# Second product of the experts in PSUM tags c and d, all row numbers read first, three decoded pairs kept in the ring

## The chip, the cores and the metric

The kernel runs on one core of one Trainium2 chip. The metric is device time in microseconds, the median of several executions of the same kernel on the same chip. One more execution is profiled; it has its own time and its own span, and every row below is from it.

## The reference

Attention over a window, then a mixture of experts with one expert for each token, then a dense layer with a squared relu:

```python
B, H, S, D = (4, 8, 576, 64)            # attention, window 128, ALiBi slopes
attn = softmax(mask(scale * q @ k.T + bias)) ; x = (attn @ v).transpose(0, 2, 1, 3).reshape(2304, 512)
expert_idx = np.argmax(x @ w_gate, axis=1)              # 8 experts, softmax weight gate_w
for e in range(8):
    mask = expert_idx == e
    h = np.maximum(x[mask] @ w1[e], 0.0)                # 512 -> 1024
    out[mask] = gate_w[mask, None] * (h @ w2[e])        # 1024 -> 512
r = np.maximum(out @ w_in, 0.0)                         # moe2: 512 -> 2048
y = (r * r) @ w_out                                     # 2048 -> 512
```

All inputs are float32 but `w_in` and `w_out`, which come as 64-bit floats and are decoded on the chip. Products are made of float16 halves, a high and a low part of each operand.

## The kernel before

The program has three stages: attention to about 160 us of the span, the eight experts from about 180 to 402 us, and the dense layer, called moe2 here, to the end. It is written as one stream of instructions for tiles; a scheduler sorts it into one queue for each engine, and each engine works through its queue in order. A tile of a pool waits until the last reader of the buffer's former tile is done.

Pools and buffers that the change touches:

- PSUM has four tags a, b, c, d with two banks each (`psum`, L131).
- `wr` (`ring`, L116) is a ring of 12 buffers for split weights, `rw` (`raw`, L128) has 4 buffers for raw loads, `xg` 6 buffers for gathered rows. `dec` is one buffer in which 64-bit words are decoded.
- `wi_s` holds the decoded `w_in` in 8 tiles, `wi_3345` to `wi_3352` in the rows. Until its own data is made, the last four also serve as staging: for raw expert weights (`stage`, L761) and for decoded pieces of `w_out` on their way to DRAM.

An expert e works as follows. `prep` (L986) reads the row numbers of its tokens from a list in DRAM into `idt`, `gather` (L993) clips them on POOL and fetches the rows by indirect DMA into `xg`. `turn` (L998) transposes each block of rows on TensorE into tag d (`transpose_x`, L791), and ACT copies it to `xt`. `s1` (L798) makes the first product in eight pieces fc with banks from a and b in turn; ACT and DVE take each result to float16 halves (L807, L808). `s2` (L849) adds up the second product over the same eight pieces in four accumulators, of tags c, c, a, b, and ACT copies them to `yT` after the last piece (L863). Weights come by SP's queue (`raw_w`, L756); ACT makes the high half (L778) and DVE the low half (L779) of each of the four pieces of `w1` and of `w2`.

Between these steps, at places named by a table (`STEPS`), the program decodes `w_in` and `w_out`: `wide` (L936) ends the step before and begins the next. A step of `w_out` (`out_step`, L916) loads 512 KB, decodes it on DVE (L880 to L882) and splits it (ACT L927, DVE L928). Eight steps are first: their results, of the list `SENT`, go into staging parts of `wi_3349` to `wi_3352`, are stored in DRAM (`wod`, L931) and are fetched when moe2 begins (`fetch_out`, L966). Then come sixteen steps of `w_in` and eight of `KEPT`, whose results stay in ring buffers.

The rows for the first experts are read late in the routing: `prep(0)` and `prep(1)`, then `gather(0)` and `gather(1)`, then three late scatters that put the gate's weights of the last tokens into the list; `prep(e + 2)` and `gather(e + 2)` are called in `then` during the second product of expert e. In moe2, `wide1` (L1191) makes 2 or 4 ring buffers of squared values for a group of 256 tokens (L1210, L1211).

Of the kernel before, what the change touches and what calls it, by code (L numbers as in the profile page):

```python
# [56 lines left out]
SENT = (4, 5, 12, 13, 6, 7, 14, 15)  # L57
# [36 lines left out]
class K:  # L94
# [754 lines left out]
    def s2(self, ws, hts, at, n, then=None):  # L849

        nc = self.nc
        ys = [self.psum(t, [P, n]) for t in "ccab"]
        for fc in range(8):
            hh, hl = hts[fc][:, 0, :n], hts[fc][:, 1, :n]
            for d, py in enumerate(ys):
                o = fc % 2 * DM + d * P
                wh, wl = (ws[fc // 2][:, a, o:o + P] for a in range(2))
                nc.tensor.matmul(py, wh, hh, start=fc == 0, stop=False)  # L858
                nc.tensor.matmul(py, wl, hh, start=False, stop=False)  # L859
                self.last_mm = nc.tensor.matmul(py, wh, hl, start=False, stop=fc == 7)  # L860
            if fc == 7:
                for d, py in enumerate(ys):
                    nc.scalar.copy(self.yT[:, d, bass.ds(at, n)], py)  # L863
            if then is not None and fc % 2 == 1:
                then(fc // 2)
# [50 lines left out]
    def out_step(self, fc):  # L916

        nc = self.nc
        f = self.wide_load(self.wo, [(slice(fc * P, (fc + 1) * P), lambda r, k: r, DM, lambda st, k: st)])

        def finish():
            if fc in KEPT:
                dst = self.wo_s[fc]
            else:
                dst = self.wi_s[4 + SENT.index(fc) % 4].rearrange("p k a c -> p (k a c)")[:, 2048:3072].rearrange(
                    "p (a d) -> p a d", a=2)
            nc.scalar.activation(dst[:, 0], f, AF.Copy, scale=WOSC)  # L927
            nc.vector.scalar_tensor_tensor(dst[:, 1], f, WOSC, dst[:, 0], op0=ALU.mult, op1=ALU.subtract)  # L928
            if fc not in KEPT:
# [20 lines left out]
    def open_wide(self, stack):  # L950
# [4 lines left out]
        self.steps = [(self.out_step, fc) for fc in SENT] + \  # L955
# [16 lines left out]
    def experts(self, stack):  # L972
# [31 lines left out]
        prep(1)  # L1004
# [11 lines left out]
        for e in range(E):  # L1016
# [10 lines left out]
            for fc in range(8):  # L1027
# [10 lines left out]
                if fc in (3, 5, 7) and more:  # L1038
                    turn(nxt, e + 1, fc // 2 - 1)
# [3 lines left out]
            def then(d):  # L1043
                if more:
                    w[2, e + 1, d] = self.load_w(2, e + 1, d)
                if e + 2 < E:
                    if d == 0:
                        prep(e + 2)
# [9 lines left out]
                if d == 3 and e < 7:  # L1058
                    self.columns(e)
                    if e == 6:  # L1060
                        self.columns(7)

            self.narrow = e == 6
# [127 lines left out]
    def wide1(self, G, m, between=lambda k: None):  # L1191
# [9 lines left out]
        g = self.gts[G, m] = [self.ring(F16, [P, 2, 8 * P]) for _ in range(n)]  # L1201
# [178 lines left out]
    def moe2(self):  # L1380
        NG, tc = NT // GT, self.tc
        self.overflow()
        nrm = {1: self.norm(1, 7168, None)}
        next(nrm[1])
# [106 lines left out]
```

## Time and profile before

| | |
|---|---|
| median of 3 runs | 748.61 us (748.33, 748.61, 751.21) |
| profiled execution | 751.45 us, span 749.6 us |
| PE busy | 712.6 us (95%) |
| weight loads (PEld) | 603.5 us (81%) |
| DVE busy | 576.8 us (77%) |
| ACT busy | 468.8 us (63%) |
| POOL busy | 206.5 us (28%) |
| mean granted clock of TensorE | 0.984 |

A busy time is the sum of an engine's instructions, and matmuls overlap each other, so that PE's 95% is no measure of waits: those stand in the waits and in the brackets of the timeline. A bracket such as `[1.82 <-DVE work L808]` says how long the engine stood idle before the row, and which instruction or transfer ended the wait. In the windows the granted clock is a share of full speed: 1.0 is 2.4 GHz and 0.5 is 1.2 GHz. The 1.8 us between the profiled time and the span lie before and after the span. The profiled execution is 2.84 us above the median of the runs.

### The profile page before, as it was taken

The numbers are of one execution on the slowest core, as the hardware profiler recorded it, in microseconds if no ns is written. First come the engines' busy times: TensorE is split into PE (matmuls) and PEld (weight loads), VectorE is DVE, ScalarE is ACT, GpSimd is POOL, SyncE is SP. The second block draws the span as 40 slices with busy tenths as digits, with TensorE's granted clock in tenths as the row PEclk, the third lists the DMA queues.
The fourth block names the chain that finished last, engine by engine and source line by source line (L and its number), as shares of the span: only waits on it lengthen the run. The fifth ranks groups of instructions, "written<-read, shape, count | busy, mean of one in ns | idle before, by whom it ended". The sixth has DMA issues, their size and how long they took to land. (4 is left out here: it accounts for less than half of the span.)

```text
span 749.6 us, 19619 instructions
## 1 busy us (share of the span) xinstructions
PE 712.6 (95%) x7979; PEld 603.5 (81%) x7979; DVE 576.8 (77%) x1442; ACT 468.8 (63%) x772; POOL 206.5 (28%) x247
## 2 busy tenths in 40 slices
PE   6899999999888999999999999999999999999996
PEld 5799899888655666788898566677899999999995
DVE  5788888864778999969986966758678787878672
ACT  5688888943457655657555664656657575757561
POOL 4573522345252401000000245523411111111011
PEclk9899999989999999999999999999999999999998
DMA  8798203876899887367704000000000000000000
GB/s 299 289 365 234 81 29 68 278 163 172 239 305 299 283 263 240 125 220 241 241 5 141 31 26 6 2 30 1 30 2 30 2 30 2 30 2 30 2 30 29
DMA packets 37416, 91.71 MB, mean 122 GB/s; under 512 B 5305, under 2 KB 16075, under 8 KB 37307
## 3 DMA queue, kind: packets, MB, share of 16 engines
q1 hardware_dynamic: 31563, 75.77, 32.1%
q0 software_dynamic: 5760, 14.65, 6.0%
q8 instruction: 64, 1.05, 0.6%
q14 instruction: 29, 0.24, 0.1%
HBM read 77.54 MB, written 13.04 MB: 121 GB/s over the span
## 5 line engine op out<-in xcount | busy, mean ns | idle before, releaser
L1187 PEld LDWEIGHTS <-wi 128*128 128x128 f16 x3024 | 170.6, 98 | 3.6 <-issue 2.3
L1323 PEld LDWEIGHTS <-wr 128*128 128x128 f16 x1008 | 98.1, 98 | 12.1 <-issue 0.7
L1187 PE MATMUL ps_a<-work,wi 128*128 128x128 f16 x1344 | 84.2, 219 | 0.0
L1187 PE MATMUL ps_b<-work,wi 128*128 128x128 f16 x1272 | 79.7, 219 | 0.4 <-ACTq L1075 0.4
L1211 DVE TENSOR_TENSOR wr<-work,wr 128x1024 f16<-128x1024 f32 (+1 forms) x72 | 70.4, 1001 | 11.0 <-ACT wr L1210 10.8
L1215 ACT ACTIVATE work<-work 128x1024 f32<-128x1024 f32 x36 | 38.1, 1057 | 54.8 <-DVE work L1207 54.8
L315 PE MATMUL ps_a<-yT,wr 128*128 128x192 f32 (+2 forms) x288 | 66.6, 352 | 5.4 <-DMA wr<-in_q_dram 5.2
L1210 ACT CAST wr<-work 128x1024 f16<-128x1024 f32 (+1 forms) x72 | 59.9, 832 | 17.1 <-DVE work L1230 7.6
L327 ACT ACTIVATE pb<-pb,nm 128x192 f32<-128x192 f32 (+2 forms) x144 | 56.5, 433 | 11.6 <-DVE nm L320 10.8
L320 DVE CUSTOM_DVE_ANT_0 pb<-ps_a,bias 128x192 f32<-128x192 f32 (+2 forms) x144 | 44.4, 327 | 16.1 <-PE ps_a L315 10.2
L778 ACT ACTIVATE wr<-rw 128x1024 f16<-128x1024 f32 x40 | 42.2, 1058 | 22.1 <-DMA rw<-in_w_dram 21.5
L1351 POOL DMA_INDIRECT out_dram<-o,oid x18 | 25.8, 1436 | 102.0 <-ACT o L1349 67.4
L779 DVE SCALAR_TENSOR_TENSOR wr<-rw,wr 128x1024 f16<-128x1024 f32 x40 | 48.8, 1221 | 5.0 <-ACT wr L778 5.0
L315 PEld LDWEIGHTS ps_a<-yT,wr 128*128 128x128 f32 x288 | 47.1, 206 | 6.4 <-DMA yT<-in_k_dram 5.5
L1286 POOL TENSOR_TENSOR yT<-wr 128x512 f32<-128x512 f16 x8 | 10.4, 1294 | 148.9 <-ACTq L1075 116.0
L338 PE MATMUL ps_b<-cst,pb 128*128 128x128 f32 x256 | 45.1, 288 | 0.5 <-ACT pts L342 0.4
L804 PE MATMUL ps_a<-work,wr 128*128 128x352 f16 (+4 forms) x112 | 34.1, 304 | 7.0 <-ACT yT L863 5.6
L1216 ACT ACTIVATE work<-work 128x1024 f32<-128x1024 f32 x36 | 38.0, 1057 | 1.1
L787 POOL DMA_INDIRECT xg<-xd,idx x21 | 26.8, 1274 | 35.6 <-PE ps_d L795 26.5
L1235 DVE TENSOR_TENSOR work<-work 128x512 f32<-128x512 f32 x18 | 13.3, 739 | 29.8 <-ACT work L1204 29.8
L859 PEld LDWEIGHTS <-wr 128*128 128x128 f16 x288 | 28.2, 98 | 9.8 <-issue 2.6
L858 PE MATMUL ps_c<-work,wr 128*128 128x352 f16 (+5 forms) x128 | 35.9, 283 | 0.0
(307 smaller groups left out, 2005.8 us busy)
## 6 DMA issues: line engine op xcount, KB each, us to landing
rw<-in_w_dram SPq DMA_DIRECT2D x40, 512.0 KB, 5.4
wi<-in_w_dram SPq DMA_DIRECT2D x20, 512.0 KB, 5.0
rw<-in_wo_dram SPq DMA_DIRECT2D x16, 512.0 KB, 4.7
rw<-in_wi_dram SPq DMA_DIRECT2D x32, 256.0 KB, 5.2
wr<-in_q_dram SPq DMA_DIRECT2D x14, 512.0 KB, 12.8
xd<-xhl POOLq DMA_DIRECT2D x16, 256.0 KB, 7.8
rw<-in_v_dram SPq DMA_DIRECT2D x12, 325.0 KB, 6.4
yT<-in_k_dram SPq DMA_DIRECT2D x4, 576.0 KB, 8.7
```

The lines of the kernel that those rows point to most:

```text
L315: nc.tensor.matmul(ps[:, s, first:hi], q[g, u, hh // 4][:, hh % 4, s if u < 4 else 0, :], self.kt[g, hh // 2][:, hh % 2, key0:key0 + hi - ...
L320: self.last_ttr = nc.vector.tensor_tensor_reduce(out=pb[:, s, first:hi], in0=ps[:, s, first:hi], in1=self.bias[:, hh, first - lo:192], sca ...
L327: self.last_exp = nc.scalar.activation(pb[:, s, first:hi], pb[:, s, first:hi], AF.Exp, bias=nm[:, s:s + 1], scale=-1.0)
L338: nc.tensor.transpose(pt[:, t, :, s, :], pb[:, s, t * P:(t + 1) * P], self.idf)
L778: self.nc.scalar.activation(t[:, 0], st, AF.Copy, scale=sc)
L779: self.nc.vector.scalar_tensor_tensor(t[:, 1], st, sc, t[:, 0], op0=ALU.mult, op1=ALU.subtract)
L1187: self.nc.tensor.matmul(ps[:, j], w[:, kp, a, w0 * P:(w0 + 1) * P], v[:, 2 * x + kp], start=kp + b == 0, stop=kp == 1 and b == 2)
L1210: self.end_act = self.fin_act = nc.scalar.copy(hi, src)
L1211: self.end_dve = self.fin_dve = V.tensor_tensor(lo, src, hi, op=ALU.subtract)
L1215: nc.scalar.activation(ci, ci, AF.Relu)
L1216: nc.scalar.activation(ci, ci, AF.Square, scale=0.5)
L1323: nc.tensor.matmul(ps[n], x[:, v, j], y[j][:, w], start=m + i + j == 0, stop=m == 1 and i == 2 and j == 3)
```

## The change

Seven edits:

1. `s2` uses tags c, c, d, d; `s1` has a and b alone, and the transposes share d with `s2`.
2. From expert 1 on, the transposes for the next expert follow pieces 2, 4 and 6 of `s1` instead of 3, 5 and 7.
3. `prep` is called for all eight experts at the start, ahead of both gathers and of the late scatters.
4. The copies of the row lists (`columns`) are called at the end of experts 5 and 6.
5. Six decoded pieces of `w_out`, the list `HELD`, are written straight to three buffers of the ring, which they keep; only pieces 14 and 15 are stored in DRAM and fetched again. Nine ring buffers are left for the experts' weights.
6. For the later groups of moe2, three of four buffers of squared values come from `rw`.
7. `wide1(0, 0)`, which is made in expert 7, uses banks a and b alone.

```diff
-SENT = (4, 5, 12, 13, 6, 7, 14, 15)
+HELD = (4, 5, 12, 13, 6, 7)
+SENT = (14, 15)
...
-        ys = [self.psum(t, [P, n]) for t in "ccab"]
+        ys = [self.psum(t, [P, n]) for t in "ccdd"]
...
+        if fc in HELD and fc not in self.wo_s:
+            for _ in self.wo_tiles((fc, fc + 1), lambda: self.ring(F16, [P, 2048])):
+                pass
...
-            if fc in KEPT:
+            if fc not in SENT:
...
-            if fc not in KEPT:
+            if fc in SENT:
...
-        self.steps = [(self.out_step, fc) for fc in SENT] + \
+        self.steps = [(self.out_step, fc) for fc in HELD + SENT] + \
...
-        prep(1)
+        for e in range(1, E):
+            prep(e)
...
-                if fc in (3, 5, 7) and more:
-                    turn(nxt, e + 1, fc // 2 - 1)
+                if more and fc in ((3, 5, 7) if e == 0 else (2, 4, 6)):
+                    turn(nxt, e + 1, (fc + 1) // 2 - (2 if e == 0 else 1))
...
-                    if d == 0:
-                        prep(e + 2)
...
-                if d == 3 and e < 7:
-                    self.columns(e)
-                    if e == 6:
-                        self.columns(7)
-
-            self.narrow = e == 6
+                if d == 3:
+                    for f in {5: range(6), 6: (6, 7)}.get(e, ()):
+                        self.columns(f)
+
+            self.narrow = e >= 6
...
-        g = self.gts[G, m] = [self.ring(F16, [P, 2, 8 * P]) for _ in range(n)]
+        spare = 3 if n == 4 and m == 0 else 0
+        g = self.gts[G, m] = [self.ring(F16, [P, 2, 8 * P]) for _ in range(n - spare)] + \
+            [self.rw.tile([P, 2048], F16, tag="rw", name="rw").rearrange("p (a n) -> p a n", a=2) for _ in range(spare)]
...
+        self.narrow = False
```

The order of instructions moves on three queues of which the prediction speaks. Line numbers of the changed kernel are 1 higher than before up to about L916 and 3 to 4 higher behind it.

POOL, from the row numbers to the first gathers (`ids` is the list in DRAM, `idx` the clipped row numbers, `xd` the rows). Before:

```order
L989 DMA ids<-ids 128x2
L989 ISA
L989 DMA ids<-ids 128x3x2
L995 TENSOR_SCALAR idx<-ids 128x1
L787 DMA xg<-xd,idx 128x1024
L995 TENSOR_SCALAR idx<-ids 128x3
L787 DMA xg<-xd,idx 128x1024 x3
```

Now, from the fourth reading on:

```order
L993 DMA ids<-ids 128x3x2
L993 ISA
L993 DMA ids<-ids 128x3x2
L993 ISA
L993 DMA ids<-ids 128x2x2
L993 ISA
L993 DMA ids<-ids 128x2x2
L993 ISA
L993 DMA ids<-ids 128x2x2
L999 TENSOR_SCALAR idx<-ids 128x1
L999 TENSOR_SCALAR idx<-ids 128x3 x3
L788 DMA xg<-xd,idx 128x1024 x4
```

Six more readings, and the clipping for experts 2 and 3, now stand ahead of the first gather; two gathers for expert 2 follow the late scatters at once.

SP, the loads and stores while expert 1's second weights are fetched (`rw` and `wi_3349` receive raw weights, `wod` receives decoded `w_out`). Before, from the store of the fifth decoded piece to that of the seventh:

```order
L931 DMA wod<-wi_3349 128x1024
L756 ISA
L756 DMA rw<-in_w_dram 128x1024
L931 DMA wod<-wi_3350 128x1024
L756 ISA
L756 DMA rw<-in_w_dram 128x1024
L756 ISA
L756 DMA rw<-in_w_dram 128x1024
L756 ISA
L756 DMA rw<-in_w_dram 128x1024
L931 DMA wod<-wi_3351 128x1024
L756 ISA
```

Now:

```order
L757 DMA rw<-in_w_dram 128x1024
L935 DMA wod<-wi_3349 128x1024
L757 ISA
L757 DMA wi_3349<-in_w_dram 128x1024
L876 DMA rw<-in_wi_dram 128x2x256 x2
L757 ISA
L757 DMA rw<-in_w_dram 128x1024
L935 DMA wod<-wi_3350 128x1024
L876 DMA rw<-in_wi_dram 128x2x256 x2
L757 ISA
L757 DMA wi_3350<-in_w_dram 128x1024
```

Before, `wi_3349` and `wi_3350` were stored for the last time several loads ahead of their use as staging; now the store of each stands one or a few rows ahead of the load into it.

ACT, the last rows ahead of the copies to `yT` of expert 1. Before:

```order
L778 ACTIVATE wr<-wi_3352 128x1024
L911 ACTIVATE wi_3345<-dec 128x896
L778 ACTIVATE wr<-rw 128x1024
L778 ACTIVATE wr<-wi_3349 128x1024
L863 ISA
L863 COPY yT<-ps_c 128x384
```

Now:

```order
L779 ACTIVATE wr<-wi_3352 128x1024
L912 ACTIVATE wi_3345<-dec 128x896
L864 ISA
L864 COPY yT<-ps_c 128x384
L864 ISA
L864 COPY yT<-ps_c 128x384
L864 ISA
L864 COPY yT<-ps_d 128x384
```

Two splits of expert 2's second weights, which stood ahead of the copies, now follow them.

## Rows read from the trace of the kernel before

**Rows 1.** waits of TensorE: engine line waited for: us in total, times, longest us

```profile
PE ps_a L804 <- ACT yT L863: 5.6, 4, 2.1
...
PE ps_d L795 <- DMA xg<-xd,idx: 3.8, 2, 3.4
...
PE ps_b L858 <- DVE work L808: 2.2, 2, 1.8
```

**Rows 2.** stages: us, PE PEld DVE ACT POOL busy (x), PEclk, DMA share, GB/s

```profile
195.50:236.80 41.30, 36.11 (x230) 21.68 (x228) 31.50 (x50) 22.25 (x32) 18.82 (x25) 0.96 0.94 304
236.80:269.80 33.00, 30.89 (x212) 20.09 (x211) 31.87 (x64) 21.83 (x32) 10.46 (x8) 0.95 0.83 275
...
348.50:372.20 23.70, 22.73 (x221) 20.10 (x220) 22.77 (x44) 14.77 (x25) 0.00 (x0) 1.00 0.79 249
372.20:402.50 30.30, 28.10 (x360) 27.68 (x360) 24.17 (x43) 17.37 (x33) 0.00 (x0) 1.00 0.07 21
402.50:470.00 67.50, 64.24 (x730) 46.30 (x731) 49.09 (x84) 37.70 (x50) 26.18 (x26) 1.00 0.16 56
```

**Rows 3.** TensorE timeline, expert stage: start us, us, line, tiles [idle before <-releaser]

```profile
206.21 0.72 PE L795 MATMUL ps_d<-id,xg 128*128 128x128 f16 x8 [3.37 <-DMA xg<-xd,idx]
...
220.38 0.32 PE L858 MATMUL ps_b<-work,wr 128*128 128x384 f16 x1 [1.82 <-DVE work L808]
...
240.37 0.31 PE L804 MATMUL ps_a<-work,wr 128*128 128x352 f16 x1 [2.11 <-ACT yT L863]
...
273.50 0.31 PE L804 MATMUL ps_a<-work,wr 128*128 128x352 f16 x1 [1.41 <-ACT yT L863]
...
373.78 0.26 PE L804 MATMUL ps_a<-work,wr 128*128 128x224 f16 x1 [1.66 <-ACT yT L863]
```

**Rows 4.** windows around three waits: us, PE busy, granted clock (1 is full speed)

```profile
206.20:210.00 3.80, 3.79 (x19) 0.55 0.87 251
...
240.40:244.10 3.70, 3.70 (x14) 0.54 0.57 150
...
273.50:277.00 3.50, 3.50 (x24) 1.00 0.92 250
```

**Rows 5.** POOL timeline, start of the experts

```profile
169.60 1.42 POOL L989 DMA_DIRECT2D ids<-ids  x2 [4.65 <-DMA ids<-tok,pos]
174.97 0.24 POOL L995 TENSOR_SCALAR idx<-ids 128x1 uint32<-128x1 f32 x1 [3.95 <-DMA ids<-ids]
175.76 1.07 POOL L787 DMA_INDIRECT xg<-xd,idx  x1 [0.56 <-POOL idx L995]
...
195.30 0.82 POOL L989 DMA_DIRECT2D ids<-ids  x1 [8.01 <-DMA ids<-tok,pos]
...
201.35 1.06 POOL L787 DMA_INDIRECT xg<-xd,idx  x1 [0.36 <-POOL idx L995]
```

**Rows 6.** TensorE timeline, start of the experts

```profile
180.92 0.62 PE L795 MATMUL ps_d<-id,xg 128*128 128x128 f16 x8 [0.45 <-DMA xg<-xd,idx]
```

**Rows 7.** ACT timeline, experts 0 and 1

```profile
182.48 0.63 ACT L927 ACTIVATE wi<-dec 128x512 f16<-128x512 f32 x1
...
225.41 1.06 ACT L778 ACTIVATE wr<-wi 128x1024 f16<-128x1024 f32 x1 [3.43 <-DMA wi<-in_w_dram]
...
239.09 0.84 ACT L863 COPY yT<-ps_c 128x384 f32 x2
```

**Rows 8.** SP timeline, the DMA issues of expert 1

```profile
207.96 0.39 SPq L756 DMA_DIRECT2D wi<-in_w_dram  x1
...
219.21 1.29 SPq L756 DMA_DIRECT2D wi<-in_w_dram  x1
```

**Rows 9.** DMA issues: count, KB each, median us from issue to landing

```profile
wod<-wi SPq DMA_DIRECT2D x8, 256.0 KB, 4.7
...
ids<-ids POOLq DMA_DIRECT2D x4, 3.0 KB, 5.4
```

## The prediction, on record before the changed kernel ran

> **What bounds the kernel now.** I read the waits of TensorE first, because its queue is full from end to end and the time is its matmuls plus its waits and slow stretches. In the experts stage three kinds of wait hold nearly all of what this change can reach [rows 1]: the first product waits for the copies to `yT` (5.6 us in four waits), the transposes wait for gathered rows (3.8 us in two), and the second product waits for DVE to free bank b (2.2 us in two). The windows by stage say what surrounds them [rows 2]. In expert 1 the DMA engines are busy 0.94 of the time and DVE 31.5 of 41.3 us; in expert 2 DVE is busy 31.9 of 33.0 us; from 402 us on PE is the bound (64.2 of 67.5 us), and there the change does nearly nothing.
>
> The timeline shows the five large waits singly [rows 3]: 3.37 us for rows of expert 2 at 206.2, 1.82 us at 220.4, 2.11 us at 240.4, 1.41 us at 273.5 and 1.66 us at 373.8, together 10.4 us. Behind two of them the granted clock falls from its upper level of 2.4 GHz to about 1.2 GHz: 0.55 over 3.8 us behind the first and 0.54 over 3.7 us behind the third, but 1.00 behind the wait of 1.41 us [rows 4]. Each dip costs 3.8 x 0.45 = 1.7 us of work. So all that could go is 10.4 + 3.4 = 13.8 us. The question is how much of it is only cover for something that is late anyway.
>
> **Start of the experts: the row numbers.** Two readings took POOL 1.42 us, the first was waited for 3.95 us, and the first gather was issued at 175.76 [rows 5]. Now eight readings stand first. POOL needs 8 x 0.75 = 6 us for them, until 175.6. That alone moves the gather by 0.6 us, for POOL used to sit idle here. But the clipping for experts 2 and 3 also stands ahead of the first gather, so it waits until the fourth reading has landed. That one is issued at about 172 and lands 3.95 [rows 5] to 5.4 us later [rows 9], so about 177.2. With 0.8 us for the last clipping and the gap that follows, the gather goes out at 178.0, 2.2 us later. TensorE was already waiting 0.45 us for gathered rows at 180.9 [rows 6], so little hides this: I take **+1.9 us**, between 0.6 (POOL's time alone) and 4.3 (a landing of 8.01 us, the longest wait for this list in the trace [rows 5]). What it buys: the reading for expert 2 was issued only at 195.3, behind the late scatters, and its first gather at 201.35 [rows 5]; two of the three gathers now go out at about 190, and the 3.37 us with its dip, **-5.1 us**, goes.
>
> **Expert 1: the decoded pieces in the ring.** The ACT half of the first `w_out` step ran at 182.48 [rows 7] into a staging tile that was free. Now it needs a ring buffer, and the first comes free when the first pair of pieces of expert 0's first product is done, about 3.7 us after that product begins (181.4 before). Eight steps go one behind another through the one `dec` buffer, so the steps, and behind them on ACT and DVE the splits of expert 1's second weights, come about 3.6 us later. On ACT the copy of the last transposes for expert 2 stands among these splits, and until it is done they hold the second d bank, which the second product now needs. I put that copy at 219.3. The wait of 1.82 us for bank b, which ended at 220.38 [rows 3], so becomes a wait for bank d that ends about 1.1 us sooner and is longer (TensorE arrives some 5 us earlier), and may bring a dip of 1.7 us with it. Up to here the gain is between -1.1 and +0.6 us.
>
> **Expert 2: the stores.** Six of eight stores of 256 KB go. The two that are left now stand right ahead of raw loads into the same tiles: the loads issued at 207.96 and 219.21 [rows 8] must wait until the store has landed, 4.7 us [rows 9]. With the 3.6 us of the steps ahead I put them at 216 and 223.5. ACT's split at 225.41 waited 3.43 us for the first of these loads [rows 7]; it comes at 228 to 230.5. Behind it on ACT stand five more splits and then the copies to `yT`, which began at 239.09 [rows 7]; two splits of 1.06 us that stood ahead of them now follow. So the first d bank is copied between 238.5 and 242.3, and only then can the transposes behind piece 2 start. Piece 4 of expert 2 begins at 244.3 to 247.8, against 246.07 before. I take the middle: at this point the change is worth **0 us**, between -1.8 and +1.7, and the first three waits with their dips have been eaten by the chain of loads and splits behind them.
>
> Against that stands the traffic: six stores of 256 KB are 1.57 MB, 5.2 us at the 304 GB/s of a stage in which the DMA engines are busy 0.94 of the time [rows 2]. SP's issues wait for free buffers more than for the engines, so I take **-1.0 us** of it, between 0 and -5.2.
>
> The trace's store lands in 4.7 us. The Trainium skill (DMA: Bandwidth & Descriptors, Anatomy of one DMA) puts a transfer at some 2.0 us plus its bytes at 436 GB/s, most of it the write receipt, which makes an estimated 2.6 us for 256 KB; by that the two loads would be 2.1 us sooner and the whole sum -4.5 us. The measured 4.7 us decides here.
>
> **Experts 3 to 7.** The waits for the copies at 273.5 (1.41 us) and in expert 6 (the fourth of [rows 1], 5.6 - 2.11 - 1.41 - 1.66 = 0.4 us) go, since `s1` has a and b for itself; the transposes behind piece 2 ask for d about 1.7 us later than the old wait began, when the copies are done or nearly so: **-1.9 us**, between 0 and -2.2. Expert 7's 1.66 us goes too, but a step of `KEPT` w_out slips from before the copies of expert 6 to behind them, on a DVE that had 24.2 us to do in 30.3 us and now gets up to 5 more [rows 2], and bank a is still held there by the norm's product. I take **+0.5 us** in all, between -1.7 and +1.5.
>
> **At nothing** stand: three fetches fewer at the start of moe2 and three buffers from `rw` for later groups (a PE-bound stage), the copies of the lists (POOL is idle beyond 240 us), and `wide1(0, 0)` in two tags, as DVE paces it. If `rw` came free late, a wait there would be new.
>
> **Sum:** 0 - 1.0 - 1.9 + 0.5 = -2.4 us. Against the profiled execution that is 751.45 - 2.4 = 749.05 us; that execution lies 2.84 us above the median of 748.61, so I predict **746.2 us**. About 0.5%, 3.7 us, is what a measurement of this kernel can tell from no change.
>
> **Rivals.**
> *The engines of the DMA were the bound.* For: 0.94 busy, and the waits of ACT for loads in expert 1 are long. Against: loads are issued when a buffer comes free. Then the 5.2 us come off the chain in full: -2.4 - 4.2 = -6.6 us, 742.0, and down to 739 if the d copies keep up too. 0.27.
> *The waits only change their name.* DVE is nearly full in experts 2 and 6 (31.9 of 33.0 and 22.8 of 23.7 us) [rows 2]; PE would wait for DVE's half of each piece instead of the copies. Then nothing comes of experts 3 to 6 and of the relief: 0 + 0.5, 749.1, no change. 0.15.
> *The row numbers make the start late, and the kernel slower.* In order on POOL, the first gather waits for the fourth reading. If that lands 8.0 us after its issue as in [rows 5], the gather goes at 180.4, TensorE is late by 4.4 instead of 1.9 us and a dip of 1.7 us follows: 4.2 us more. The ring buffers come free with the same matmuls, so the chain moves with it and no later slack takes it back; with the chain at its late end (+1.7) and no relief (+1.0) the sum is +4.5 us, 753.1. It decides from a first gather behind 180 on; at 178 it is covered. 0.13.
> That the change does not do what it says (a, b still shared) is excluded by the order of the queues shown with it.
>
> **Numbers.** The forecast has 0.45, with a range of its own from 743.5 to 749.5. The 8-in-10 range leaves out the lowest part of the first rival and the upper half of the last: 740.5 to 751.0. Faster by over 0.5% (under 744.9): most of the first rival, 0.26, and a quarter of the forecast, 0.11, with 0.02 of the second: 0.39. Slower by over 0.5% (above 752.3): most of the last, 0.09, and 0.02 of the rest: 0.11. Within: 0.50.
>
> **What would show it.** Right: the first gather at about 178; no wait for rows at expert 2's transposes; a wait of the second product for bank d until about 219; the wait of `s1` for `yT` gone from the list, with one of the transposes for `yT` in its place at about 241; piece 4 of expert 2 at 246 ± 2 us. The forecast is wrong if expert 2 begins more than 3 us sooner (the first rival), if waits for DVE take up the gain from expert 3 on (the second), or if the first gather comes behind 180 (the last).

## The result: slower, and the profile after

The changed kernel takes 756.51 us (median of 754.93, 755.77, 757.25 and 759.49), the kernel before 749.91 us in the runs beside it (748.33 to 751.58): a ratio of 1.0103, with a 95% interval from 1.0077 to 1.0128. That is slower by 1%, and outside the predicted range (740.5 to 751.0 us). The profiled execution took 754.93 us, span 753.1, the fastest of the four; against the first profiled execution it is 3.5 us longer.

The waits of TensorE, changed kernel, to be read against [rows 1] (engine, line waited for: us in total, times, longest us):

```profile
PE ps_a L805 <- DVE work L809: 6.4, 2, 3.5
...
PE ps_d L859 <- ACT work L797: 4.0, 2, 3.9
PE ps_a L805 <- DVE yT L1143: 3.4, 1, 3.4
...
PE ps_d L796 <- DMA xg<-xd,idx: 0.9, 1, 0.9
...
PE ps_d L796 <- ACT yT L864: 0.6, 1, 0.6
```

What the change was to remove is gone: the first product waits for no copy to `yT`, the transposes wait for gathered rows for 0.9 us only, at the start of the experts, and the second product not at all for DVE. Others stand in their place: the copy of transposes out of tag d (L797, 4.0 us in two), and on DVE its half of a piece of the first product (L809, 6.4 us in two) and the product of the first norm (L1143, 3.4 us).

The TensorE timeline gives the four large waits, against [rows 3] (start us, us, line, tiles [idle before <-releaser]):

```profile
216.61 0.48 PE L859 MATMUL ps_d<-work,wr 128*128 128x384 f16 x1 [3.85 <-ACT work L797]
...
303.44 0.29 PE L805 MATMUL ps_a<-work,wr 128*128 128x304 f16 x1 [2.88 <-DVE work L809]
...
356.06 0.37 PE L805 MATMUL ps_a<-work,wr 128*128 128x256 f16 x1 [3.50 <-DVE work L809]
...
379.76 0.35 PE L805 MATMUL ps_a<-work,wr 128*128 128x224 f16 x1 [3.43 <-DVE yT L1143]
```

And windows behind each of them, against [rows 4] (us, PE busy, granted clock, DMA share, GB/s):

```profile
216.60:220.40 3.80, 3.79 (x12) 0.50 0.70 194
...
303.40:307.00 3.60, 3.56 (x23) 0.64 0.26 61
...
356.00:359.60 3.60, 3.54 (x25) 0.58 0.52 154
...
379.70:383.30 3.60, 3.54 (x21) 0.55 0.63 249
```

All four are followed by the lower clock level for most of 3.6 to 3.8 us. Taken as the share of full speed that is missing, that is 1.9, 1.3, 1.5 and 1.6 us of work. In the kernel before, two waits were followed by a dip [rows 4].

Where the time went is seen best from the start of each expert's first product on TensorE's timeline:

| us of the span | before | after | difference |
|---|---|---|---|
| expert 1 | 194.88 | 194.29 | -0.6 |
| expert 2 | 234.52 | 233.64 | -0.9 |
| expert 3 | 268.34 | 263.51 | -4.8 |
| expert 4 | 299.86 | 293.75 | -6.1 |
| expert 5 | 325.66 | 324.15 | -1.5 |
| expert 6 | 348.66 | 346.00 | -2.7 |
| expert 7 | 373.78 | 373.87 | +0.1 |
| moe2 | 403.27 | 407.23 | +4.0 |

So the change does gain 6 us, by expert 4. Three waits of 2.88, 3.50 and 3.43 us in experts 4, 6 and 7, with 4.4 us of work lost to the slow clock behind them, give back over 10. By stages, against [rows 2] (us, then PE, PEld, DVE, ACT, POOL busy, clock, DMA share, GB/s):

```profile
194.00:231.00 37.00, 33.15 (x209) 19.73 (x207) 29.18 (x45) 19.74 (x31) 12.74 (x15) 0.91 0.85 282
231.00:263.00 32.00, 32.00 (x231) 21.27 (x229) 30.85 (x67) 21.17 (x31) 3.87 (x3) 1.00 0.83 280
263.00:295.60 32.60, 32.35 (x236) 21.65 (x235) 28.28 (x49) 19.65 (x31) 4.01 (x3) 1.00 0.62 199
...
345.00:375.00 30.00, 25.95 (x241) 22.68 (x240) 25.05 (x47) 18.77 (x32) 0.00 (x0) 0.94 0.71 223
```

In the stage of expert 1 the DMA engines are now 0.85 busy, not 0.94. DVE is not fuller than before; in the stage of the wait at 356 it has 25.0 of 30.0 us to do, against 22.8 of 23.7 [rows 2]. It is late, not overloaded.

**Why DVE is late in expert 4.** ACT's and DVE's timelines of the changed kernel at the wait, first ACT, then DVE:

```profile
294.63 1.08 ACT L779 ACTIVATE wr<-rw 128x1024 f16<-128x1024 f32 x1
300.90 0.95 ACT L912 ACTIVATE wi<-dec 128x896 f16<-128x896 f32 x1 [5.18 <-DVE dec L907]
301.75 0.41 ACT L808 ACTIVATE work<-ps_a 128x304 f16<-128x304 f32 x1
```

```profile
288.28 1.22 DVE L780 SCALAR_TENSOR_TENSOR wr<-wi,wr 128x1024 f16<-128x1024 f32 x1
...
293.65 1.22 DVE L780 SCALAR_TENSOR_TENSOR wr<-wi,wr 128x1024 f16<-128x1024 f32 x1
297.93 0.43 DVE L881 TENSOR_SCALAR dec<-rw 128x512 uint32<-128x512 uint32 x1 [3.06 <-DMA rw<-in_wi_dram]
...
302.92 0.47 DVE L809 SCALAR_TENSOR_TENSOR work<-ps_a,work 128x304 f16<-128x304 f32 x1
```

ACT stood still for 5.18 us. It had reached the ACT half of a `w_in` step (L912), which waited for DVE's decode, and DVE's decode (L881) had waited 3.06 us for its load. Behind L912 in ACT's queue stood the relu of expert 4's first piece (L808), whose result had long been in bank a; DVE's half (L809) followed at 302.92. The same step before, the tenth of `w_in` in both kernels, on ACT:

```profile
301.73 0.95 ACT L911 ACTIVATE wi<-dec 128x896 f16<-128x896 f32 x1 [2.06 <-DVE dec L906]
...
304.22 0.42 ACT L807 ACTIVATE work<-ps_a 128x304 f16<-128x304 f32 x1
```

It ran at 301.73, 0.8 us later than now, and waited 2.06 us. TensorE had come 6 us forward, the step had not. Its load was issued at 290.50, right behind a load of expert weights (SP's timeline of the changed kernel; the rows at 207 belong to a point below):

```profile
207.51 0.34 SPq L935 DMA_DIRECT2D wod<-wi  x1
208.05 0.34 SPq L757 DMA_DIRECT2D wi<-in_w_dram  x1
...
289.52 0.34 SPq L757 DMA_DIRECT2D wi<-in_w_dram  x1
...
290.50 1.21 SPq L876 DMA_DIRECT2D rw<-in_wi_dram  x2
```

That load of weights (289.52) stood 7.3 us on SP. The profile puts the wait down to DVE, and the split of a staged buffer (L780, from 288.28 to 289.50) ended just as the load went out. So there is a loop through three queues that each work in order: a step waits for its load, the load stands on SP behind a load of weights, that one waits for a split, and the split stands on ACT and DVE behind the step before. The loads of `w_in` went out at 270.1, 279.8, 286.5 and 293.5 before, one in 7.8 us on average; now at 271.6, 281.0, 290.5 and 299.8, one in 9.4.

**Why DVE is late in expert 6.** DVE's timeline of the changed kernel:

```profile
354.11 0.43 DVE L881 TENSOR_SCALAR dec<-rw 128x512 uint32<-128x512 uint32 x1 [0.75 <-DMA rw<-in_wi_dram]
354.45 1.22 DVE L780 SCALAR_TENSOR_TENSOR wr<-rw,wr 128x1024 f16<-128x1024 f32 x1
355.59 0.42 DVE L809 SCALAR_TENSOR_TENSOR work<-ps_a,work 128x256 f16<-128x256 f32 x1
```

ACT's relu of the piece had begun at 353.35. DVE's half of it stood behind the first row of a decode, which waited for its load, and behind a split.

**Why DVE is late in expert 7.** DVE's timeline, changed kernel, then before:

```profile
375.68 0.43 DVE L881 TENSOR_SCALAR dec<-rw 128x512 uint32<-128x512 uint32 x1 [0.38 <-DMA rw<-in_wo_dram]
...
376.75 1.22 DVE L780 SCALAR_TENSOR_TENSOR wr<-rw,wr 128x1024 f16<-128x1024 f32 x1
...
378.49 1.21 DVE L1143 TENSOR_TENSOR yT<-yT,ps_a 128x1024 f32<-128x1024 f32 x1
```

```profile
374.14 0.69 DVE L881 SCALAR_TENSOR_TENSOR dec<-rw,dec 128x512 uint32<-128x512 uint32 x1
...
375.47 1.21 DVE L1141 TENSOR_TENSOR yT<-yT,ps_a 128x1024 f32<-128x1024 f32 x1
```

The norm's product frees bank a for piece 2 of expert 7. It stands behind the decode of a `w_out` step and a split and came at 378.49, against 375.47 before.

### The profile page after: what moved, and what is told of

Read it like the earlier page. It is cut to its first block, busy times and chain, and to the rows that moved or that the text cites. A ratio compares the mean times of both kernels' runs of the same rounds, so it can differ in the third digit from the quotient of the medians.

```text
span 753.1 us, 19622 instructions
## 1 busy us (share of the span) xinstructions
PE 712.0 (95%) x7979; PEld 601.8 (80%) x7979; DVE 577.5 (77%) x1442; ACT 467.4 (62%) x772; POOL 200.4 (27%) x247
## 5 line engine op out<-in xcount | busy, mean ns | idle before, releaser
L1189 PE MATMUL ps_b<-work,wi 128*128 128x128 f16 x1320 | 82.7, 219 | 0.3 <-PEq L1077 0.3
L316 PE MATMUL ps_a<-yT,wr 128*128 128x192 f32 (+2 forms) x288 | 65.0, 346 | 5.5 <-DMA wr<-in_q_dram 5.3
L1327 PEld LDWEIGHTS <-wr 128*128 128x128 f16 x648 | 63.4, 98 | 8.2 <-issue 0.7
L1215 DVE TENSOR_TENSOR wr<-work,wr 128x1024 f16<-128x1024 f32 (+1 forms) x48 | 48.8, 1037 | 11.2 <-ACT wr L1214 11.0
L1290 POOL TENSOR_TENSOR yT<-wr 128x512 f32<-128x512 f16 x10 | 12.7, 1267 | 167.2 <-ACTq L1077 128.3
L780 DVE SCALAR_TENSOR_TENSOR wr<-rw,wr 128x1024 f16<-128x1024 f32 x40 | 48.7, 1218 | 5.2 <-ACT wr L779 5.1
L1355 POOL DMA_INDIRECT out_dram<-o,oid x18 | 23.6, 1309 | 103.3 <-ACT o L1353 46.0
L1214 ACT CAST wr<-work 128x1024 f16<-128x1024 f32 (+1 forms) x48 | 42.5, 885 | 8.2 <-DVE work L1234 4.2
L859 PE MATMUL ps_d<-work,wr 128*128 128x352 f16 (+5 forms) x128 | 36.5, 288 | 4.0 <-ACT work L797 4.0
L860 PEld LDWEIGHTS <-wr 128*128 128x128 f16 x288 | 28.5, 99 | 12.3 <-issue 5.4
L1327 PEld LDWEIGHTS <-rw 128*128 128x128 f16 x360 | 34.8, 98 | 3.8
L788 POOL DMA_INDIRECT xg<-xd,idx x21 | 24.4, 1164 | 46.5 <-PE ps_d L796 25.5
```

The lines of the kernel that those rows point to most:

```text
L316: nc.tensor.matmul(ps[:, s, first:hi], q[g, u, hh // 4][:, hh % 4, s if u < 4 else 0, :], self.kt[g, hh // 2][:, hh % 2, key0:key0 + hi - ...
L780: self.nc.vector.scalar_tensor_tensor(t[:, 1], st, sc, t[:, 0], op0=ALU.mult, op1=ALU.subtract)
L1189: self.nc.tensor.matmul(ps[:, j], w[:, kp, a, w0 * P:(w0 + 1) * P], v[:, 2 * x + kp], start=kp + b == 0, stop=kp == 1 and b == 2)
L1214: self.end_act = self.fin_act = nc.scalar.copy(hi, src)
L1215: self.end_dve = self.fin_dve = V.tensor_tensor(lo, src, hi, op=ALU.subtract)
L1327: nc.tensor.matmul(ps[n], x[:, v, j], y[j][:, w], start=m + i + j == 0, stop=m == 1 and i == 2 and j == 3)
```

## The experiments

Ratios are to the kernel before on the same chip, in runs taken beside each other. The kernel before itself had medians from 748.8 to 752.5 us on the chips used, so that times from different chips are not compared. The changed kernel was timed on one chip, in the four executions above, and not again beside its variants. Theories, in short: 1, the ring of nine buffers makes loads and steps late; 2, the new order of copies and steps on ACT, which comes with the banks, makes the waits. The expected microseconds were given for a kernel before of 749 to 750 us.

### The parts alone

**Without the held pieces** (edits 5 and 6 undone, all else kept):

```diff
-HELD = (4, 5, 12, 13, 6, 7)
-SENT = (14, 15)
+SENT = (4, 5, 12, 13, 6, 7, 14, 15)
...
```

> The changed kernel with eight w_out pieces stored and fetched as before and all 12 ring buffers for the experts' weights (buffers of the later groups of moe2 from the ring again); banks, early transposes and early row numbers stay. Theory 1 (the ring of 9 makes splits, loads and so the w_in steps late): 739 to 744 us, 6 to 10 less than before, the three new waits of 2.9 to 3.5 us in experts 4, 6 and 7 gone. Theory 2 (the new order of copies and w_in steps on ACT, which comes with the banks, makes the waits): 753 to 758 us, the waits stay.

Measured: 759.23 us, ratio 1.0108 (1.0054 to 1.0163). Theory 1 fails as the whole answer: with all twelve buffers back the kernel is as slow as with nine. Its waits, and one of them on TensorE's timeline:

```profile
PE ps_d L858 <- ACT work L796: 6.6, 4, 4.0
PE ps_a L804 <- DVE work L808: 5.5, 5, 2.9
...
PE ps_a L804 <- DVE yT L1139: 3.2, 1, 3.2
```

```profile
244.06 0.31 PE L804 MATMUL ps_a<-work,wr 128*128 128x352 f16 x1 [2.92 <-DVE work L808]
```

But the time goes elsewhere. In experts 4 and 6, where the changed kernel waited 2.88 and 3.50 us for DVE, no such wait is over 1 us here, as theory 1 had it. Expert 2 takes 38.5 us from start to start instead (changed kernel 29.9, before 33.8), with waits of 2.9 us for DVE and 2.1 us for a copy of transposes. Of the four large waits, those for the copy of transposes in expert 1 (4.0 us) and for the norm in expert 7 (3.2 us) are in both.

**Held pieces alone** (edits 5 and 6 on the kernel before):

> The kernel before with the six pieces kept in the ring and nothing else but the buffers of moe2 that this needs. Theory 1: 753 to 760 us, w_in steps from the eighth on 4 to 8 us later, in experts 4 to 7 new waits of TensorE for DVE. Theory 2: 747 to 751 us, no such waits.

Measured: 755.56 us, ratio 1.0065 (1.0039 to 1.0091), with waits of 1.8 us for DVE in expert 4 and 4.5 us for a copy to `yT` in expert 6. Loads of `w_in` at 270.8, 280.4, 289.4, 298.6, the cadence of the changed kernel. Theory 1 holds for this part.

**Banks and transposes alone** (edits 1, 2 and 7 on the kernel before):

```diff
-        ys = [self.psum(t, [P, n]) for t in "ccab"]
+        ys = [self.psum(t, [P, n]) for t in "ccdd"]
...
-                if fc in (3, 5, 7) and more:
...
+                if more and fc in ((3, 5, 7) if e == 0 else (2, 4, 6)):
...
-            self.narrow = e == 6
+            self.narrow = e >= 6
...
```

> The kernel before with c, c, d, d, the earlier transposes and the narrow first product of moe2 in expert 7. Theory 1: 744 to 748 us; the waits for the copies to yT go, the wait for gathered rows of expert 2 stays or grows by the piece that the transposes come sooner. Theory 2: 752 to 757 us with new waits in experts 4 to 7.

Measured: 757.10 us, ratio 1.0102 (1.0049 to 1.0156). Here loads of `w_in` are not late (326.7 and 353.5 for the thirteenth and the sixteenth, 326.1 and 353.0 before). Its waits:

```profile
PE ps_d L795 <- DMA xg<-xd,idx: 4.0, 1, 4.0
...
PE ps_d L858 <- ACT work L796: 3.4, 2, 3.1
PE ps_a L804 <- DVE yT L1141: 3.1, 1, 3.1
```

The rows of expert 2 are waited for 0.6 us longer, as the transposes ask sooner; the second product waits 3.1 us for a copy of transposes out of tag d, in expert 2; the norm's wait of 3.1 us in expert 7 is there. Theory 2 had the time about right, and of its new waits in experts 4 to 7 the norm's is the only large one: most of the loss is in expert 2, which takes 37.1 us against 33.8 before.

**Row numbers alone** (edits 3 and 4 on the kernel before):

```diff
-        prep(1)
+        for e in range(1, E):
+            prep(e)
...
-                    if d == 0:
-                        prep(e + 2)
...
```

> The kernel before with all row numbers read at the start and the list copies late. Both theories: the wait of 3.37 us for rows of expert 2 and its slow stretch go. Theory 1: 744 to 748 us, of which some is given back at the copies of expert 1. Theory 2 says the same here or no change, 747 to 750 us.

Measured: 752.86 us, ratio 1.0040 (1.0015 to 1.0065). The 3.37 us for rows go, and the second product of expert 1 waits for DVE instead, 3.5 us at 216.9 and 1.4 us at 219.4. Both theories expected a gain or no change; every part alone costs.

**The ring alone** (the kernel before with three ring buffers held idle from the start of the experts to expert 6):

```diff
+        full = [self.ring(F16, [P, 2048]) for _ in range(3)]
+        for t in full:
+            nc.gpsimd.memset(t[:, :2], 0.0)
...
+            if e == 6:
+                m7 = xgs[7][0].shape[0]
+                for t in full:
+                    nc.gpsimd.tensor_copy(t[:m7, 2:4], xgs[7][0][:, :2])
```

> The kernel before with three ring buffers taken out of use from the start of the experts to expert 6 (each is written once and read once) and nothing else: stores, banks and row numbers as before. If the smaller ring is what makes the w_in loads late in the kernel with held pieces alone: 752 to 758 us, and the loads of w_in from the ninth on are issued 4 to 8 us later, some 9 us apart. If it is the order of steps around the held pieces: within 2 us of 749.6, and the loads as before.

Measured: 753.61 us, ratio 1.0064 (1.0043 to 1.0084), as the held pieces alone. Loads of `w_in` at 271.2, 281.4, 291.9, 298.9, so one in 9.2 us. TensorE, then ACT, in expert 4:

```profile
305.81 0.41 PE L804 MATMUL ps_a<-work,wr 128*128 128x304 f16 x1 [5.35 <-ACT yT L863]
```

```profile
304.11 0.95 ACT L911 ACTIVATE wi<-dec 128x896 f16<-128x896 f32 x1 [5.65 <-DVE dec L906]
...
305.30 0.45 ACT L863 COPY yT<-ps_a 128x352 f32 x1
```

Three buffers fewer make the loop longer, with stores and everything else as before. The held pieces alone, which spare six stores besides, cost the same (1.0065). TensorE lost 5.35 us at one place, because ACT waited 5.65 us for a decode ahead of the copy to `yT`.

### The order of the steps

From here theory A says that a decode step ahead of TensorE's work in an in-order queue makes the waits, and theory B that the weights' buffers are the bound.

**The norm first** (the changed kernel; DVE's part of the `w_out` steps from the end of expert 6 on ordered behind the norm's product):

```diff
+                    if e == 7:
+                        with tc.issue_after(self.nmul.ins):
+                            wide()
...
+                    if (e, d) == (6, 3):
+                        with tc.issue_after(self.nmul.ins):
+                            wide()
...
-        V.tensor_tensor(y, y, sb.unsqueeze(1).to_broadcast([P, 4, GW]), op=ALU.mult)
+        self.nmul = V.tensor_tensor(y, y, sb.unsqueeze(1).to_broadcast([P, 4, GW]), op=ALU.mult)
```

> The changed kernel with one order fixed: in expert 7 the product of the first norm on DVE (which frees bank a for the third piece) stands ahead of the DVE work of the w_out steps that are called from there on. Theory A (a decode step ahead of TensorE's work in an in-order queue makes each new wait): the wait of 3.4 us at 376 us of the span shrinks to under 1 us and its slow stretch goes, 752 to 754 us, 3 to 4.5 less than the changed kernel. Theory B (the weights' buffers are the bound, and a wait taken away comes back at the next split): the time stays within 1 us of 756.5.

Measured: 753.45 us, ratio 1.0067 (1.0037 to 1.0096), against 1.0103 without. The wait at 376 us is gone from the timeline; 0.7 us for DVE at 386.7 is what remains in the first product of expert 7; the wait in expert 6 is 4.2 us here, and TensorE waits 2.0 us at the start of moe2. So the wait went as theory A had it. That the time fell with it is not shown, as the two intervals overlap (1.0037 to 1.0096 and 1.0077 to 1.0128).

**Steps behind each piece** (the changed kernel; a step that is called between two pieces of the first product is ordered behind ACT's and DVE's work on that piece):

```diff
-        nc.scalar.activation(ht[:, 0], ph, AF.Relu)
-        nc.vector.scalar_tensor_tensor(ht[:, 1], ph, 0.0, ht[:, 0], op0=ALU.max, op1=ALU.subtract)
+        self.ra = nc.scalar.activation(ht[:, 0], ph, AF.Relu)
+        self.rd = nc.vector.scalar_tensor_tensor(ht[:, 1], ph, 0.0, ht[:, 0], op0=ALU.max, op1=ALU.subtract)
...
-                    wide()
+                    if e > 0:
+                        with tc.issue_after(self.ra.ins), tc.issue_after(self.rd.ins):
+                            wide()
+                    else:
+                        wide()
```

> The changed kernel with the w_in and w_out steps that are called between the pieces of the first product held behind ACT's and DVE's work on that piece, in experts 1 to 7. Theory A: the waits for DVE of 2.9 us in expert 4 and 3.5 us in expert 6 go with their slow stretches, 747 to 751 us, the steps themselves no earlier. Theory B: waits for splits of the weights or for later pieces take their place, 754 to 758 us.

Measured: 746.31 us, ratio 0.9964 (0.9941 to 0.9987), 1.4% under the changed kernel's 1.0103. Between 242 and 346 us of the span TensorE has no wait of over 0.4 us. ACT in expert 4:

```profile
295.32 0.42 ACT L808 ACTIVATE work<-ps_a 128x304 f16<-128x304 f32 x1
296.87 0.42 ACT L808 ACTIVATE work<-ps_b 128x304 f16<-128x304 f32 x1 [1.13 <-PE ps_b L807]
297.19 0.94 ACT L912 ACTIVATE wi<-dec 128x896 f16<-128x896 f32 x1
```

The relus of both pieces now come ahead of the step, and the step finds its input ready. The steps and their loads are no sooner: loads eight to eleven of `w_in` go out one in 9.8 us, the tenth step runs on ACT at 313.1 (changed kernel: 300.9), and TensorE does not wait for it. So it is the place of the steps in the queue, and not their lateness, that stopped TensorE. What is left is a wait of 2.6 us for DVE in expert 6, with the 2.9 us for the copy of transposes in expert 1 and 2.1 us for the norm:

```profile
PE ps_a L805 <- DVE work L809: 3.0, 2, 2.6
PE ps_d L859 <- ACT work L797: 2.9, 1, 2.9
...
PE ps_a L1146 <- DVE sd L1141: 2.8, 3, 2.1
```

**The same order without the change** (the same diff on the kernel before):

> The kernel before with the same order of steps behind each piece, as a control. Theory A: within 2 us of the kernel before (748 to 751 us), since its waits are for copies and rows and not for steps. Theory B: the same; if it gains over 3 us, the order of the steps is worth as much without the change as with it.

Measured: 747.00 us, ratio 0.9992 (0.9969 to 1.0016). The order is worth nothing that can be measured to the kernel before. Both theories had expected that; what the run rules out is that the order gains as much without the change as with it.

**Both orders** (both diffs on the changed kernel; in expert 7 only the step behind piece 1 is ordered behind the norm's product):

> The changed kernel with both orders fixed: steps behind ACT's and DVE's work on the piece, and the norm's product ahead of the w_out steps of expert 7. If the two remedies act on different waits, the wait of 2.6 us in expert 6 stays and the time is 744 to 747 us; the norm's place is already right with the steps behind, so at most 1 us under the kernel with steps behind alone (746.3).

Measured: 747.71 us, ratio 0.9980 (0.9957 to 1.0003). Nothing is added to the steps' order, which already puts the norm in its place.

**The steps' order with parts of the change.** Six kernels put the same order on parts of the change; their diffs are those above, put together, and in the last one the transposes follow pieces 3, 5 and 7 again.

> Banks, early transposes and early row numbers, with eight stores and 12 ring buffers as before, and the steps behind each piece. Theory A (the order of the steps made the 759 us of this kernel without it, not the stores): 743 to 748 us. If the stores and the loads behind them bound this kernel: 752 to 758 us.

> The kernel before with c, c, d, d, the earlier transposes, the narrow first product in expert 7 and the steps behind each piece; row numbers, stores and ring as before. Theory A: 745 to 749 us; the waits of 2.2 us for DVE in expert 2 and 3.1 us in expert 7 go, the 4.0 us for gathered rows stays. If the shared tag d costs by itself (transposes against accumulators): a wait of 3 us for the copy of transposes stays in expert 2, 750 to 754 us.

> Held pieces, early row numbers and steps behind each piece, with the old banks (c, c, a, b) and the transposes after pieces 3, 5, 7. If the parts add up as in the kernels with steps behind so far (banks and steps 752.9 against 747.0 for steps alone, so banks +5.9): 741 to 744 us. If the three parts only work together: 747 to 753 us.

> Held pieces and steps behind each piece alone. If the ring of 9 costs by itself: 750 to 755 us, w_in loads some 9 us apart in experts 2 and 3. If it cost only through the order of the steps: 745 to 748 us, at or under the kernel before with steps behind (747.0).

> Early row numbers and steps behind each piece alone. If the wait for rows of expert 2 (3.3 us and a slow stretch) is a real gain once the steps are out of the way: 743 to 746 us. If the second product's banks take it back as in the kernel with early row numbers alone (waits of 3.5 and 1.4 us for DVE): 747 to 750 us.

> The changed kernel with steps behind each piece, but the transposes again after pieces 3, 5 and 7. If the earlier transposes only ask for rows and copies too soon: 742 to 746 us, with the wait of 2.9 us for bank d at expert 1's second product longer by one piece at most. If they are needed to free bank d for the second product: 748 to 753 us, that wait 4 to 6 us and more of them.

Measured, as ratios to the kernel before, with the 95% interval:

| what of the change | order as scheduled | steps behind each piece |
|---|---|---|
| nothing | 1.0003 (0.9977 to 1.0030) | 0.9992 (0.9969 to 1.0016) |
| held pieces | 1.0065 (1.0039 to 1.0091) | 1.0003 (0.9979 to 1.0026) |
| row numbers | 1.0040 (1.0015 to 1.0065) | 1.0018 (1.0000 to 1.0036) |
| banks, early transposes | 1.0102 (1.0049 to 1.0156) | 1.0052 (1.0023 to 1.0081) |
| all but held pieces | 1.0108 (1.0054 to 1.0163) | 1.0056 (1.0019 to 1.0093) |
| all but banks and transposes | not run | 0.9997 (0.9968 to 1.0027) |
| all, transposes late again | not run | 0.9992 (0.9967 to 1.0017) |
| all | 1.0103 (1.0077 to 1.0128) | 0.9964 (0.9941 to 0.9987), again 1.0001 (0.9978 to 1.0024) |

In every row that has both, the middle value falls with the order, by 0.1 to 1.4%, but clear of the intervals only for the held pieces and for the whole change. The held pieces cost nothing that can be measured once the order is set, so the smaller ring costs through the order, as far as these intervals tell. The banks without the held pieces keep half a per cent, as the second expectations of `no_held_behind` and `banks_behind` said and theory A did not: the kernel with banks and order still waits 3.2 us for DVE and 2.1 us for the copy of transposes in expert 2, and 2.2 us for the norm in expert 7. The expected 741 to 744 us for held pieces and row numbers without the banks did not come (a ratio of 0.9997): the costs of parts do not add up. For the row numbers and for the late transposes it was the expectation without a gain, too, that came.

The profiles say where the parts act. From the start of expert 1 to that of expert 3 the ten with held pieces take 67.4 to 70.5 us, the ten without 69.8 to 77.3, and the three longest of them have the banks (75.2, 76.5 and 77.3). From expert 3 to moe2 the four with nine ring buffers and the steps as scheduled (the last one with the norm first) take 143.8, 146.0, 141.8 and 141.7 us, all others 134.9 to 140.5. Two profiles of one kernel differ by up to 1.3 us in the first stretch and up to 2.0 in the second. So the held pieces gain in experts 1 and 2, and the ring that they leave loses more from expert 3 on, where the order of the steps is not set.

**The kernel before once more**, for the spread of its profile:

> The kernel before once more, for the spread of its profile: the same waits for gathered rows (2.7 to 3.4 us) and copies (1 to 2 us), 748 to 751 us; the start of the experts within 2 us of the first profile.

Measured: 750.00 us, ratio 1.0003. From the first piece of expert 0 to moe2 it took 221.8 us, as in the first profile (221.9); the changed kernel takes 226.8, and the one with steps behind each piece 217.8, but 223.0 in its repeat below. Counted from expert 0, the two profiles of the kernel before agree within 0.8 us at the start of every expert; the two of the steps' order differ by up to 5.2 us, so that a single profile decides nothing finer than that.

**One step moved**, and the steps' order once more beside it:

```diff
-         ((3,), (1, 3)), ((3,), (1, 3)),
+         ((3,), (1,)), ((1, 3), (1,)),
```

> The changed kernel with steps behind each piece, and one step moved: from the end of expert 5's second product to behind piece 1 of expert 6, the last of expert 6 to expert 7. If a step ahead of TensorE's work is also what makes the remaining wait of 2.6 us in expert 6: that wait goes, a ratio of 0.990 to 0.995 to the kernel before. If it is the splits of the weights: the wait stays and the ratio is 0.995 to 1.000.

> The changed kernel with steps behind each piece once more, beside the one with a moved step on the same chip: a ratio of 0.994 to 0.999 to the kernel before if the 0.996 of the first time is the kernel's and not the chip's.

The first of these kernels does not compute the layer. It decodes the last piece of `w_out` into `dec` (to 428.0 us), and the second norm writes over `dec` (L1154 to L1157, 429.1 to 430.4 us) before the piece is split (L932, 430.66). Measured: ratio 1.0036 (1.0017 to 1.0056) with the step moved, 1.0001 (0.9978 to 1.0024) without. That is outside both ranges that were expected. TensorE in expert 6 without and with the moved step, and in expert 7 with it:

```profile
353.88 0.37 PE L805 MATMUL ps_a<-work,wr 128*128 128x256 f16 x1 [3.14 <-DVE work L809]
```

```profile
354.33 0.27 PE L805 MATMUL ps_a<-work,wr 128*128 128x256 f16 x1 [1.17 <-DVE work L809]
...
382.03 0.35 PE L805 MATMUL ps_a<-work,wr 128*128 128x224 f16 x1 [6.61 <-DVE yT L1147]
```

The wait in expert 6 falls from 3.14 to 1.17 us, so a step called at the end of the second product made most of it. But the steps then run into expert 7, where the norm's product waits for them: 6.61 us. The kernel is no remedy. The repeat of the steps' order is level with the kernel before; the 0.36% of the first time did not come again, and both intervals overlap between 0.9978 and 0.9987. What is shown twice is that the order takes back the loss, not that the whole is faster than before. A version that surely beats the kernel before was not found.

## Why the prediction was wrong

- **Start of the experts, +1.9 us: right in size.** The changed kernel's POOL timeline, against [rows 5]:

```profile
167.31 5.07 POOL L993 DMA_DIRECT2D ids<-ids  x7 [4.09 <-DMA ids<-tok,pos]
...
175.14 1.06 POOL L788 DMA_INDIRECT xg<-xd,idx  x1 [0.26 <-issue]
```

  From the first reading to the first gather it took 7.8 us, against 6.2 before, so +1.7, where I had 2.2 for the gather. The readings of this execution began 2.3 us sooner, which hides it: the first piece of expert 0 came at 180.5, against 181.4 and 180.5 in two profiles of the kernel before. The third rival, a first gather behind 180, did not happen. Its 8.01 us was misread besides: in [rows 5] POOL stood idle until the late scatters had landed (`ids<-tok,pos`) and only then issued the reading, so that this was no reading's landing.
- **The wait for rows, -5.1 us: right.** None is left at expert 2's transposes, and expert 1's second product began 5.8 us sooner (211.13 against 216.93); 0.6 of it lay ahead of expert 1.
- **Bank d in expert 1: right in kind.** TensorE waited 3.85 us for the copy of transposes, with a dip; it ended at 216.6, and I had put it at 219.3. At expert 2 the gain was 0.9 us, inside the -1.1 to +0.6 that I gave.
- **The stores in expert 2, 0 us: wrong, to the other side.** I had the load into `wi_3349` wait until the store had landed, 4.7 us. It was issued at 208.05, 0.54 us behind the store (SP's rows above). The decoded piece and the raw weights lie in different parts of the tile, so nothing waits. A price of landing time was put on a dependence that the addresses don't have; the estimate by the Trainium skill (DMA: Bandwidth & Descriptors, Anatomy of one DMA) that stood beside it priced the same wait, and neither price was paid. That section gives its fit for transfers issued from GpSimd; these stores are issued by SP, and with 4.7 us the trace does not agree with the estimated 2.6. A reading was wrong, too: in the order of the staged loads, ACT's split at 225.41 is that of the load issued at 219.21, while the load of 207.96 was split at 217.20. In the changed kernel that split came at 225.06, where I had 228 to 230.5. So the copies to `yT` began at 235.52 and the d banks were free by 237.1, where I had the first between 238.5 and 242.3; piece 4 of expert 2 began at 241.24 and not at 246 ± 2, the transposes waited for no copy there, and expert 3 started 4.8 us sooner, not 1. The relief that I put at 1.0 us is in this. Held pieces are worth several microseconds in experts 1 and 2, as the profiles of the parts say; how much of that is the DMA engines and how much SP's queue can't be told apart.
- **Experts 3 to 7, -1.9 + 0.5 us: wrong, and this is the step that failed.** I had -1.4 us in all; they cost 8.8 us (from -4.8 at expert 3 to +4.0 at moe2). I counted the old waits as gained and looked for what the same instructions would wait for next, but not for what stood ahead of them on ACT and DVE. The steps of `w_in` and `w_out` kept a pace of their own through the loop of loads, splits and decodes; TensorE came 6 us forward and met them. On ACT the step that waited 5.18 us for its input held the relu that TensorE needed, which stood behind it.
- **The rival "the waits only change their name"** had the right place in two of the three waits (DVE's half of a piece) and the wrong price. I let the new waits take back the gain and no more. They were 2.9 to 3.5 us where the old ones in experts 4 to 7 were 0.4 to 1.7, and each brought a slow stretch of 1.3 to 1.6 us, which none of those had (clock 1.00 in the stages of experts 6 and 7 [rows 2]).
- **The held pieces.** I priced nine ring buffers in expert 1 only, where the first free buffer comes late. There it cost nothing: the first step ran on ACT at 182.5 in both kernels and waited 0.6 us, where I had it 3.6 us later. The price came from 271 us on, in the cadence of the loads, and `ring9` shows it without the rest.

The cause, then: the decode steps stand ahead of TensorE's work in the queues of ACT and DVE, in the order that the scheduler gave them, and are hidden as long as they are done before that work is due. The change sped up TensorE and, through the smaller ring, slowed the steps. Fixing that order alone takes the kernel from 1.0103 to 0.9964 and 1.0001. The banks without the held pieces lose in another place, expert 2, and cost half a per cent even with the order set; which of `ccdd`, the early transposes and the narrow product in expert 7 makes it was not tried apart, and why the held pieces take it away is open.

## What to carry to other kernels

Before counting a removed wait as gained, look up in the trace when the side work in the same in-order queues (decodes, splits, loads) runs, and whether it would come sooner too; where it wouldn't, the gain ends at the first such instruction that stands ahead. After a change that moves the consumer forward, set the order of side work against the critical instructions by hand, and only then judge the change. A ring made smaller shows in the spacing of the loads, far behind the place where the buffers are taken; whether that costs time depends on what stands in the queues behind the late steps.

## What the runs showed of the hardware

Between 178 and 412 us, in the traces of all runs, TensorE had 19 waits of 3.27 us or more, and the lower clock level followed each of them (mean granted clock of the next 3.6 us 0.50 to 0.66). Shorter waits went either way: 3.24 us in expert 2 (banks with the steps' order) and 3.14 us in expert 6 (both orders) were followed by full clock, one of 1.99 us in expert 7 (held pieces alone) by 0.55. A wait of some 3 us with a slow stretch of 1.3 to 1.6 us behind it costs some 4.5 us.

Loads of one kind on SP's queue kept a spacing of 9.2 to 9.4 us over four issues, while the DMA engines were busy 0.62 of the time in that stage of the changed kernel (263 to 296 us), and SP stood 7.3 us before a load for DVE: the queue's waits set the pace there, not the engines.

The median of the same kernel differed by 3.7 us between chips (748.8 and 752.5 us), over half of what the change cost.
